# Attention ahead of two feed-forward blocks: the values' products of two query tiles issued together every second step

## Chip, cores and metric

One core of a Trainium2 chip. The metric is the device time of one execution in microseconds; the median of three runs of the kernel before is 1003.15 us (1000.76 to 1003.25).

## What is computed

Four batches of eight heads, 576 positions, head dimension 64, everything in float32. Then two feed-forward blocks on the 2304 x 512 result.

```python
scores = q @ k.T / sqrt(64)                      # causal
scores += minimum(-(cum_i - cum_j), 0)           # cum = cumsum(max(s, 0))
attn = exp(scores - rowmax) / (rowsum + 1e-9)
x = (attn @ v)                                   # heads side by side: 2304 x 512
h = maximum(x @ w_in, 0);  x = (h * h) @ w_out   # first block, d_ff 2048
h = x @ w2_in;  out = (h * cos(h)) @ w2_out      # second block
```

## The kernel before

The tokens are cut into nine blocks of 256 queries (`ORDER`, `_segments`). The attention of block k+1 runs beside the first feed-forward block of block k: that is the loop `for k in range(NB1)`, and each of its passes is a *step*. A **unit** is a segment of queries of one batch; a **job** is one tile of at most 128 queries of one head. There are 160 jobs. Jobs 0 to 31 (heads below `EARLY`) take another path, with float32 products and transpositions by TensorE, and are not touched by the change. Jobs 32 to 159 are touched. Most units have two tiles a head, so that an even job is a head's first tile and the odd job behind it the second; jobs 48 to 55, 104 to 111 and 144 to 159 have one tile a head, a width of 576 keys, and there an even and an odd job are two heads that share an output tile. Jobs 48 to 55, 104 to 111 and the second tiles of jobs 56 to 71 and 112 to 127 have 64 queries, the others 128.

The order on each engine is the program order, written by `step(i)` (the tile framework adds semaphores alone; a tile's buffer is handed on when all that reads it is done). What happens to job j, by step:

- step j: scores on TensorE (`emit_qk`, L487 and L496) into one of three PSUM banks, two for 576 keys
- step j+1: mask and row minimum on VectorE (`emit_mask`, L510), exp on ScalarE (`emit_exp`, L527)
- step j+2: `emit_split`: VectorE writes the weights as a float16 high and low part into a tile `p` (L555, L559; where the width is no multiple of 128, GpSimd first clears the rest, L554), and SP's queue issues a DMA that transposes `p` into a tile `pt` (L565)
- step j+5 (`LAG`, `lag(i)`): `emit_pv`: the products of `pt` with the values on TensorE, three of 64 columns for each 128 keys (L590), into the PSUM bank `pvs`
- after a pair of heads is complete, in the next step: `evacuate` (VectorE divides by the row sums and reads `pvs`, `xp`, L630) and, at the step's end, `turn` (one or two transpositions on TensorE, L644)

Between these a step issues one or two *slots* of the feed-forward block: `g1` (12 products of 256 columns into `hps`, L844) or `g2` (12 into `y`, L873), with `gact` on ScalarE (L855 to L857) and `grest` on VectorE (L863, the tile `gl`) between the two. All these products and their weights are 4 bytes wide; those of L590 are 2 bytes wide. At a block's last `g2` the two halves of `y` are copied into two tiles `yst` (ScalarE and VectorE, L881), stored to DRAM from SP's queue (L882), and squared and summed on ScalarE (L884). The next block's first `g2` writes the same PSUM banks.

The buffers in question: `pt` has three; `p` has two, and from the end of the first weights' conversion every third job (i % 3 == 2) uses the single buffer `p3` in place of them (`p_tile`); the tag `stg` has two buffers of 2 KB per partition, used by the weights' conversion (before step 37 and again in the last block) and by the two `yst`.

How many steps block k gets follows from `unit_done`, which uses `lag`: block 1 runs from step 37, block 2 from step 55, block 3 from step 79. SP's queue carries, in program order, the transpositions, the loads of q and k (`raw`, L220), of the values (`vb`, L367) and the stores of `yst`.

Of the kernel before, what the change touches and what calls it, by code (L numbers as in the profile page):

```python
# [10 lines left out]
F16 = mybir.dt.float16  # L11
# [12 lines left out]
NF = DFF // 128  # L24
# [9 lines left out]
LAG = (3, 5)  # L34
# [62 lines left out]
EARLY = 16  # L97
# [17 lines left out]
def attention_moe_moe_kernel(  # L115
# [24 lines left out]
    wp = ctx.enter_context(tc.tile_pool(name="wp", bufs=1))  # L140
# [4 lines left out]
    at = at_stack.enter_context(tc.tile_pool(name="at", bufs=1, side="right"))  # L145
# [171 lines left out]
    jobs = []  # L317
# [9 lines left out]
    jd = {}  # L327
    xb = {}
    evq, xtq, xcq = [], [], []
    lag1, wrest = [], []  # L330
# [185 lines left out]
        j["sb"], j["nb"] = sb, nb[0:r, len(j["ps"]) - 1:len(j["ps"])]  # L516

    def p_tile(i):
        third = nw[2] >= 2 * NF and not wrest and i % 3 == 2
        return at.tile([128, 1280], F16, tag="p3" if third else "p", bufs=1 if third else 2, name="p")  # L520

    def emit_exp(i):
# [17 lines left out]
    def emit_split(i):  # L540
        n, ti, q, r = jobs[i]
        j = jd[i]
        w, sb = j["w"], j["sb"]
        cw = 128 * ((w + 127) // 128)
        if n < EARLY:
            pp = j["ps"][0][0][:, BT:BT + cw]
            pt = at.tile([128, 640], F32, tag="pt", bufs=3, name="pt1")
            (nc.scalar.copy if ti else nc.vector.tensor_copy)(pt[:, 0:w], pp)
            j["pt"] = pt
            yield  # L550
            return
        p = p_tile(i)
        if cw > w:
            nc.gpsimd.memset(p[0:r, 0:2 * cw].rearrange("p (a c) -> p a c", a=2)[:, :, w:cw], 0.0)  # L554
        nc.vector.tensor_scalar(  # L555
            out=p[0:r, 0:w], in0=sb[0:r, 0:w], scalar1=PSC, scalar2=None, op0=ALU.mult
        )
        yield
        nc.vector.scalar_tensor_tensor(  # L559
            out=p[0:r, cw:cw + w], in0=sb[0:r, 0:w], scalar=PSC, in1=p[0:r, 0:w],  # L560
            op0=ALU.mult, op1=ALU.subtract,
        )
        pt = at.tile([128, 1280], F16, tag="pt", bufs=3, name="pt")
        pt = pt[:, 0:2 * cw // 128 * r].rearrange("p (a r) -> p a r", r=r)
        nc.sync.dma_start_transpose(out=pt, in_=p[0:r, 0:2 * cw])  # L565
        j["pt"] = pt
        yield
# [106 lines left out]
    def job(i):  # L674
        return jobs[i] if 0 <= i < NJ else None

    def lag(i):
        return LAG[not job(i) or jobs[i][0] >= EARLY]

    def heads_ahead(i, *fs):  # L680
        if job(i) and jobs[i][1] == 0:
# [3 lines left out]
    def unit_done(u):  # L685
        return last_job[u] + lag(last_job[u]) + 3


    nw = [2, 0, 0]
    stq = [(wp, 3)]  # L690
    p3 = [0]
# [285 lines left out]
    def softmax_tail(i):  # L977
        if job(i - 1):
            yield from emit_mask(i - 1)
        for j in stage(2, i - 2):  # L980
            yield from emit_split(j)

    def step(moe=0, bits=0, attn=True):
# [37 lines left out]
        if attn:  # L1021
            for j in stage(0, i - 2):
                if jobs[j][1] == 0:
                    load_v(jobs[j][0])
            for j in stage(3, i - LAG[0]):
                if j > i - lag(j):
                    stages[3] -= 1
                    break
                emit_pv(j)
# [104 lines left out]
    while prog[0] < unit_done(0):  # L1134
        i = prog[0]
# [271 lines left out]
```

## Time and profile before

| what | value |
|---|---|
| median of the runs | 1003.15 us |
| the profiled execution | 1003.76 us, its span 1002.0 us |
| PE busy | 966.9 us (96%) |
| DVE, ACT busy | 723.9 us (72%), 655.5 us (65%) |
| products of L590 | 1296, 61.2 us busy, from 122.9 to 559.6 us |
| transpositions by DMA, L565 | 128 |

Times in the profile count from the start of the span. PE is TensorE's matmuls, PEld its weight loads, DVE VectorE, ACT ScalarE, POOL GpSimd, SP the queue from which most DMAs are issued. In a timeline each row is a start, a duration, an engine, a line, an operation and its tiles; "x9" means nine in a row merged. [...]

### The profile page before, as it was taken

How to read it: one execution, taken by the hardware profiler on the slowest of the kernel's cores; microseconds unless marked ns; L12 is line 12 of the kernel's file. 1: busy time of each engine (PE TensorE's matmuls, PEld its weight loads, DVE VectorE, ACT ScalarE, POOL GpSimd, SP SyncE). 2: the span in 40 equal slices, each digit the busy share in tenths (PEclk: the TensorE clock that was granted, in tenths of full speed). 3: DMA queues.
4: the chain of work that ended last, by engine and by line, in shares of the span. 5: the costliest groups of instructions: out<-in, count | busy, mean ns of one | idle time of the engine just before them, and what ended most of it. 6: DMA issues, size and time to landing. Idle time of an engine off the chain costs nothing.

```text
span 1002.0 us, 20487 instructions
## 1 busy us (share of the span) xinstructions
PE 966.9 (96%) x7266; PEld 740.6 (74%) x7266; DVE 723.9 (72%) x1865; ACT 655.5 (65%) x1596; POOL 163.2 (16%) x258
## 2 busy tenths in 40 slices
PE   5999899999999999999999999999999999999998
PEld 4788898899999998999999997444544454444444
DVE  6879788867777897787888267798887545555555
ACT  4789777767777777767776578777766444433433
POOL 2000011111111121111211023330033341000000
PEclk9999999999999999999999999999999999999999
DMA  8955599746887986467898569210000000011001
GB/s 268 292 182 181 118 202 203 170 111 157 196 162 160 178 193 175 109 155 145 192 206 180 188 237 360 95 43 1 1 1 1 0 1 1 0 43 43 23 20 64
DMA packets 150711, 126.65 MB, mean 126 GB/s; under 512 B 108048, under 2 KB 125792, under 8 KB 150608
## 3 DMA queue, kind: packets, MB, share of 16 engines
q1 hardware_dynamic: 146688, 119.05, 46.1%
q0 software_dynamic: 3904, 6.29, 2.5%
q8 instruction: 57, 0.93, 0.4%
q14 instruction: 46, 0.38, 0.1%
q10 hardware_dynamic: 16, 0.01, 0.0%
HBM read 85.25 MB, written 15.81 MB: 101 GB/s over the span
## 4 chain that ended last, share of the span: by engine, by line
PE 79%; DVE 8%; DMA 6%; ACT 4%; issue 2%; SPq 1%; DVEq 0%; ACTq 0%
PE hps L844 18%; PE y L873 18%; PE o L1285 17%; PE hp L1230 17%; PE qkp L496 4%; PE pvs L590 4%; DMA rw<-in_w_dram 3%; DMA raw<-in_qk_dram 1%; PE xps L644 1%; DVE st L716 1%; DVE sb L510 1%; DVE gl L863 1%; DVE wt L737 0%; DVE k L357 0%; SPq L178 0%
## 5 line engine op out<-in xcount | busy, mean ns | idle before, releaser
L844 PE MATMUL hps<-xh,wt 128*128 128x256 f32 x1152 | 241.4, 292 | 4.1 <-ACT g L855 4.0
L873 PE MATMUL y<-gh,wt 128*128 128x256 f32 x1152 | 237.7, 289 | 0.0
L844 PEld LDWEIGHTS hps<-xh,wt 128*128 128x128 f32 x1152 | 191.7, 194 | 7.0 <-ACT g L855 5.5
L873 PEld LDWEIGHTS y<-gh,wt 128*128 128x128 f32 x1152 | 189.9, 192 | 1.3
L1230 PE MATMUL hp<-yh,wt 128*128 128x512 f16 (+1 forms) x640 | 185.9, 358 | 0.0
L1285 PE MATMUL o<-wt,gh 128*128 128x512 f16 x576 | 171.3, 379 | 2.0 <-ACT wt L1300 1.9
L873 PE MATMUL y<-gl,wt 128*128 128x256 f32 x576 | 163.4, 284 | 2.6 <-DVE gl L863 2.6
L844 PE MATMUL hps<-xl,wt 128*128 128x256 f32 x576 | 164.3, 285 | 0.9 <-DVE xl L661 0.9
L1230 PEld LDWEIGHTS <-wt 128*128 128x128 f16 x960 | 92.2, 98 | 93.3
L1242 ACT ACTIVATE a<-hp,hsc 128x512 f32<-128x512 f32 (+1 forms) x80 | 51.4, 643 | 118.6 <-PE hp L1230 117.2
L855 ACT ACTIVATE g<-hps 128x256 f32<-128x256 f32 x144 | 54.6, 379 | 107.7 <-PE hps L844 105.8
L1230 PE MATMUL hp<-yl,wt 128*128 128x512 f16 (+1 forms) x320 | 114.4, 358 | 0.0
L873 PEld LDWEIGHTS y<-gl,wt 128*128 128x128 f32 x576 | 110.6, 192 | 3.7 <-DVE gl L863 3.1
L844 PEld LDWEIGHTS hps<-xl,wt 128*128 128x128 f32 x576 | 111.7, 194 | 1.4 <-DVE xl L661 1.1
L1285 PE MATMUL o<-wt,gl 128*128 128x512 f16 x288 | 109.2, 379 | 0.4 <-DVE gl L1272 0.4
L1243 DVE TENSOR_SCALAR kf<-a 128x512 f32<-128x512 f32 (+1 forms) x80 | 34.5, 431 | 103.8 <-ACT a L1242 103.4
L1285 PEld LDWEIGHTS <-gh 128*128 128x128 f16 x576 | 56.2, 98 | 66.7 <-issue 2.4
L527 ACT ACTIVATE sb<-sb,nb 128x128 f32<-128x128 f32 (+8 forms) x160 | 93.7, 586 | 12.1 <-DVE nb L510 12.0
L339 POOL DMA_DIRECT2D k<-ext_d x80 | 40.8, 510 | 341.9 <-ACT g L856 92.3
L510 DVE CUSTOM_DVE_ANT_0 sb<-qkp,mask 128x128 f32<-128x128 f32 (+8 forms) x160 | 72.7, 454 | 13.8 <-PE qkp L487 8.6
L1251 ACT ACTIVATE a<-kf 128x512 f32<-128x512 f32 (+1 forms) x80 | 46.8, 585 | 46.6 <-DVE kf L1244 46.1
L559 DVE SCALAR_TENSOR_TENSOR p<-sb,p 128x512 f16<-128x512 f32 (+7 forms) x128 | 72.4, 565 | 4.0
(119 smaller groups left out, 1680.1 us busy)
## 6 DMA issues: line engine op xcount, KB each, us to landing
rw<-in_w_dram SPq DMA_DIRECT2D x64, 512.0 KB
raw<-in_qk_dram SPq DMA_DIRECT2D x32, 352.0 KB
raw<-in_qk_dram SPq DMA_DIRECT2D x16, 384.0 KB
v_d<-vt SPq DMA_DIRECT2D x16, 320.0 KB
raw<-in_qk_dram SPq DMA_DIRECT2D x16, 320.0 KB
vb<-v_d SPq DMA_DIRECT2D x32, 160.0 KB
vr<-in_v_dram POOLq DMA_DIRECT2D x15, 320.0 KB, 4.7
y_d<-yst SPq DMA_DIRECT2D x18, 256.0 KB
```

The lines of the kernel that those rows point to most:

```text
L339: nc.gpsimd.dma_start(out=hd[n][1][64:68, BT - nq:BT + nl], in_=ext_d[n, :, BT - nq:BT + nl])
L496: nc.tensor.matmul(p[0:r, 0:cn], m[0:kk, qo:qo + r], m[0:kk, BT + c0:BT + c0 + cn], start=(kk == 128), stop=(kk == 68),)
L510: nc.vector.tensor_tensor_reduce(out=sb[0:r, c0:c0 + cn], in0=p[0:r, 0:cn], in1=mask[0:r, mo + c0:mo + c0 + cn], scale=-0.125, scalar=(3.0 ...
L527: nc.scalar.activation(out=sb[0:r, 0:w], in_=sb[0:r, 0:w], func=ACTF.Exp, scale=-1.0, bias=j["nb"], accum_out=pd[n - h % 2]["z"][0:r, ti, ...
L559: nc.vector.scalar_tensor_tensor(out=p[0:r, cw:cw + w], in0=sb[0:r, 0:w], scalar=PSC, in1=p[0:r, 0:w], op0=ALU.mult, op1=ALU.subtract,)
L844: nc.tensor.matmul(hp, w[:, a, c * 128:(c + 1) * 128], (xh, xl)[e][:, c, :], start=(n == 0), stop=(n == 3 * KD - 1),)
L855: nc.scalar.activation(out=g, in_=hp, func=ACTF.Relu)
L873: nc.tensor.matmul(yps[k][d // 2][:, d % 2, :], w[:, a, d * 128:(d + 1) * 128], (gh, gl)[e], start=(f == 0 and n == 0 and d % 2 == 0), sto ...
L1230: nc.tensor.matmul(hp, w[:, a, c * 128:(c + 1) * 128], (yh, yl)[e][:, c, :], start=(m == 0), stop=(m == 3 * KD - 1),)
L1242: nc.scalar.activation(out=a, in_=hp, func=ACTF.Copy, scale=sm["hsc"][:, j, f:f + 1], bias=0.25)
L1251: nc.scalar.activation(out=a, in_=kf, func=ACTF.Sin, scale=-6.2831850)
L1285: nc.tensor.matmul(ops[j][a], (gh, gl)[e][:, a * 128:(a + 1) * 128], w[:, x, :], start=(first and m == 0), stop=(last and m == 2),)
```

## The change

`lag` is five for an even job and four for an odd one (it was five for both), so that the products of jobs 2m and 2m+1 are both issued at the end of step 2m+5, the odd job's directly behind the even one's. The odd job's come one step earlier than before. Steps of even number issue none. Since the last job of every unit is odd, each unit is done one step earlier: block 1 has 18 steps (it had 19), the later blocks as many as before.

Three of four jobs use the three buffers of `pt`, so that a buffer comes round after four jobs. Jobs with i % 4 == 3 take theirs elsewhere: in `p3` where the keys fill more than 512 columns, else in `stg`. `p_tile` no longer takes `p3` for jobs of 576 keys.

```diff
--- before.py
+++ after.py
@@ -516,7 +516,7 @@
         j["sb"], j["nb"] = sb, nb[0:r, len(j["ps"]) - 1:len(j["ps"])]
 
     def p_tile(i):
-        third = nw[2] >= 2 * NF and not wrest and i % 3 == 2
+        third = nw[2] >= 2 * NF and not wrest and i % 3 == 2 and jd[i]["w"] <= 512
         return at.tile([128, 1280], F16, tag="p3" if third else "p", bufs=1 if third else 2, name="p")
 
     def emit_exp(i):
@@ -560,7 +560,12 @@
             out=p[0:r, cw:cw + w], in0=sb[0:r, 0:w], scalar=PSC, in1=p[0:r, 0:w],
             op0=ALU.mult, op1=ALU.subtract,
         )
-        pt = at.tile([128, 1280], F16, tag="pt", bufs=3, name="pt")
+        if i % 4 < 3:
+            pt = at.tile([128, 1280], F16, tag="pt", bufs=3, name="pt")
+        elif cw > 512:
+            pt = at.tile([128, 1280], F16, tag="p3", bufs=1, name="pt3")
+        else:
+            pt = wp.tile([128, 1024], F16, tag="stg", bufs=2, name="pt4")
         pt = pt[:, 0:2 * cw // 128 * r].rearrange("p (a r) -> p a r", r=r)
         nc.sync.dma_start_transpose(out=pt, in_=p[0:r, 0:2 * cw])
         j["pt"] = pt
@@ -675,7 +680,9 @@
         return jobs[i] if 0 <= i < NJ else None
 
     def lag(i):
-        return LAG[not job(i) or jobs[i][0] >= EARLY]
+        if job(i) and jobs[i][0] < EARLY:
+            return LAG[0]
+        return LAG[1] - (i % 2 if job(i) else 0)
 
     def heads_ahead(i, *fs):
         if job(i) and jobs[i][1] == 0:
```

## Rows read from the trace of the kernel before

**Rows 1.** The page of the profile: the span and the busy line.

```profile
span 1002.0 us, 20487 instructions
...
PE 966.9 (96%) x7266; PEld 740.6 (74%) x7266; DVE 723.9 (72%) x1865; ACT 655.5 (65%) x1596; POOL 163.2 (16%) x258
```

**Rows 2.** Busy time by stretch: us, then busy (instructions) per engine, PEclk, DMA.

```profile
150.00:200.00 50.00, 45.80 (x445) 42.12 (x445) 43.33 (x128) 36.60 (x102) 8.84 (x21) 0.97 0.83 187
196.50:199.50 3.00, 3.00 (x16) 3.00 (x17) 2.63 (x11) 1.34 (x4) 0.37 (x1) 0.52 1.02 306
200.00:250.00 50.00, 50.00 (x461) 46.26 (x460) 35.37 (x143) 36.20 (x113) 8.30 (x22) 1.00 0.54 134
```

**Rows 3.** Timeline of PE, steady stretch: start, duration, engine, line, operation, tiles.

```profile
301.78 0.28 PE L844 MATMUL hps<-xh,wt 128*128 128x256 f32 x1
301.90 0.43 PE L590 MATMUL pvs<-vb,pt 128*128 128x64 f16 x9
302.17 0.36 PE L873 MATMUL y<-gh,wt 128*128 128x256 f32 x1
302.38 0.28 PE L873 MATMUL y<-gl,wt 128*128 128x256 f32 x1
```

**Rows 4.** Timeline of PE, tiles of 64 queries.

```profile
200.90 0.28 PE L873 MATMUL y<-gh,wt 128*128 128x256 f32 x1
201.11 0.66 PE L590 MATMUL pvs<-vb,pt 128*64 128x64 f16 x15
201.70 0.38 PE L844 MATMUL hps<-xh,wt 128*128 128x256 f32 x1
201.92 0.28 PE L844 MATMUL hps<-xl,wt 128*128 128x256 f32 x1
```

**Rows 5.** Waits of SP's queue: total us, times, longest.

```profile
SPq L565 <- PE pvs L590: 81.5, 71, 3.9
```

**Rows 6.** Timeline of PE, two products that waited; idle time in brackets.

```profile
195.55 0.63 PE L590 MATMUL pvs<-vb,pt 128*64 128x64 f16 x15 [1.39 <-DVE xp L630]
...
387.27 0.63 PE L590 MATMUL pvs<-vb,pt 128*64 128x64 f16 x15 [1.11 <-DVE xp L630]
```

**Rows 7.** Timeline of PE, unit 8.

```profile
523.34 0.39 PE L844 MATMUL hps<-xh,wt 128*128 128x256 f32 x1 [1.40 <-ACT g L855]
```

**Rows 8.** Timelines of ACT, DVE and PE at step 37.

```profile
122.39 0.59 ACT L881 COPY yst<-y 128x512 f32<-128x512 f32 x1 [0.31 <-PE y L873]
123.01 0.63 ACT L884 ACTIVATE yj<-yst 128x512 bf16<-128x512 f32 x1
...
123.89 0.63 ACT L884 ACTIVATE yj<-yst 128x512 bf16<-128x512 f32 x1 [0.16 <-DVE yst L881]
...
123.11 0.69 DVE L881 COPY yst<-y 128x512 f32<-128x512 f32 x1 [3.72 <-PE y L873]
...
127.48 0.39 PE L844 MATMUL hps<-xh,wt 128*128 128x256 f32 x1 [0.47 <-ACT g L855]
```

**Rows 9.** Timelines of SP and POOL: a transposition issued, its landing awaited.

```profile
193.24 1.33 SPq L565 DMA_TRANSPOSE pt<-p  x1
...
197.62 0.37 POOL L554 MEMSET p<- 64x128 f16 x1 [2.44 <-DMA pt<-p]
```

**Rows 10.** Timelines of SP and PE, jobs 36 and 37.

```profile
131.12 4.06 SPq L565 DMA_TRANSPOSE pt<-p  x2
...
135.38 0.44 PE L590 MATMUL pvs<-vb,pt 128*128 128x64 f16 x9
...
139.14 0.52 PE L590 MATMUL pvs<-vb,pt 128*128 128x64 f16 x12
```

**Rows 11.** Timelines of DVE and PE, jobs 54 to 56.

```profile
197.64 0.21 DVE L555 TENSOR_SCALAR p<-sb 128x128 f16<-128x128 f32 x1
...
203.56 0.66 PE L590 MATMUL pvs<-vb,pt 128*64 128x64 f16 x15
...
206.44 0.66 PE L590 MATMUL pvs<-vb,pt 128*64 128x64 f16 x15
```

## Prediction

> **What bounds the kernel now.** I read the page first: TensorE is busy for 966.9 of 1002.0 us [rows 1]. That number alone proves little, since its matmuls overlap, so I read the busy time by stretch next. [...] The timeline of PE then shows what a product costs: its distance to the next start. A product of 256 columns takes 0.12 us (301.78 to 301.90), nine products of L590 take 0.27 us (301.90 to 302.17, 0.03 each) [rows 3]. Last I read who waits: SP's queue, PE's idle times, and the places where the change gives a buffer to a second kind of tile.
>
> **Fewer returns from the short products.** The first long product behind a group of L590 takes 0.21 us (302.17 to 302.38) in place of 0.12 [rows 3]: 0.09 us a return. I read this as its weights, which the 0.03 us of the last short product cannot cover. With 128 jobs issued in 64 pairs, 64 returns go. By the order in the code, 24 of them lead into a long product (every second even job of the units with two tiles a head): 24 x 0.09 = 2.2 us. The other 40 lead into the transpositions of `turn`, which the change leaves standing between long products. There part of the 0.09 us stays, since a transposition is short too and its own return is still paid. Of these, 32 have tiles of 128 queries: 0 to 0.09 each, taken at 0.02, near zero because the long product's return behind a transposition remains: 0.6 us (0 to 2.9). Eight have tiles of 64 queries, where the way in costs as well: 200.90 to 201.11 is 0.21 us, and the way out 0.22 [rows 4]. That is 0.09 + 0.10 at most; the way in goes for certain: 0.09 to 0.19 each, taken at 0.12: 1.0 us (0.7 to 1.5). Together 3.8 us (2.9 to 6.6). The number of products is unchanged.
>
> [...]
>
> **Two waits that lose their cause.** At 195.55 and 387.27 us PE sat idle for 1.39 and 1.11 us before a group of L590, until DVE had read `pvs` (L630) [rows 6]. Both are at tiles of 576 keys, where before the change a pair of heads is read out in the same step in which the next job's products are issued. After it, the read-out falls in an even step and the next products at the end of the odd step behind it, a whole step later. 2.5 us go (0 to 2.5, the lower end if DVE is then late for another reason). [...]
>
> **SP's queue stands less.** With three buffers the transposition of job j waits for the products of job j-3, which are issued later in the same step: 71 waits, 81.5 us, 1.15 us each [rows 5]. With four, job j waits for job j-4, done a step or two before. So transpositions, and the loads queued behind them on SP, start about 1 us earlier. Most of that is hidden. Where it is not: at 523.34 us PE had waited 1.40 us for ACT [rows 7]; I put it to a late load of q and k. I take 1.0 us (0 to 1.4).
>
> **The borrowed `stg` at step 37.** Job 35 takes one of the two `stg` buffers in step 37, and its products come in step 39. In step 37 the first block's `y` is copied to two `yst`. The first takes the other buffer; the second cannot wait for job 35, because the `g2` that needs the freed PSUM banks stands ahead of job 35's products on PE. It has to wait for the first `yst` to be squared and stored. Before, the copies began at 122.39 (ACT) and 123.11 (DVE) [rows 8]. The square of the first ends at about 123.7 (123.01 + 0.63 and its sum): 0.6 us later than DVE began. The store can begin at 122.98; how long it takes no row tells. The nearest landing that a row shows is a transposition issued at 193.24, awaited until 197.62: 4.4 us [rows 9]. That makes a DVE copy at up to 127.4, 4.3 us late. ACT's second square stands in its order behind that copy, and everything of ACT behind the square; PE already waits for ACT at 127.48, 0.47 us long [rows 8], so there is no cover. Cost 0.6 to 4.3 us; I take 2.4, between ends of which neither is nearer in kind. Blocks 3, 4 and 6 copy while job 75, 91 or 131 holds `stg`, but there these products come at the end of the same step, ahead of the next `g2`: about 1 us of DVE's time, beside PE's work, 0.
>
> **Odd jobs one step earlier.** Their transposed tile must have landed when the even job's products end. The tightest row is job 37: its transposition was issued at 131.12, and the even job 36 ends its products at 135.7 (135.38 and nine times 0.03), 4.6 us later; job 37's own began at 139.14 [rows 10]. With a landing after 4.4 us [rows 9] nothing is lost; if it landed only just before 139.14, 3.4 us. I take 1.0 (0 to 3.4), the lower end being nearer. Elsewhere a step of 2.9 to 3.8 us between two groups [rows 10, 11] and the earlier issue leave enough: 0.
>
> **`p3` held past its turn.** Job 55 (576 keys) keeps its transposed tile in `p3` until its products in step 59; job 56 wants `p3` for `p` in step 58. DVE then stands, with its masks, `gl` and read-outs queued behind, from 197.64 until job 55's products, which follow job 54's: 203.56 + 2 x 0.59 = 204.7 [rows 4, 11]. That is up to 7.1 us of DVE's time by the old clock. What PE issues in these two steps (two slots of 12 x 0.12 = 1.44 us, two pairs of scores, the products: some 4.6 us) needs only what DVE made before, because `grest` is issued about three steps ahead of its `g2`. So PE loses little if it then finds DVE no more than that behind: 0 to 7.1 us. Job 113 stands the same way behind job 111, but within one step, 0 to 2.4 us. Both together I take at 1.4 us, near the lower end, since after 200 us DVE has 35.37 us of work in 50 [rows 2] and catches up. The two-buffer `p` at 576 keys costs 0: job j-2's transposition was issued two steps before.
>
> **Sum.** -3.8 - 2.5 - 0.5 - 1.0 + 2.4 + 1.0 + 1.4 = -3.0 us. Block 1's lost step changes nothing by itself, since its slots stay. On the profiled execution (1003.76 us, 1.8 more than its span) this gives 1000.8; that one lies 0.6 above the median of 1003.15, to which I forecast 1000.2 us.
>
> **Rivals.**
> - *The gain is real but given back.* Step 37 at 4.3 and job 37 at 3.4 us take 4.3 us more than I did, and the net is +1.3, with the earlier SP queue and the clock still in: 1004.5. For it: no cover at 127.48 [rows 8]. Against: one place each.
> - *DVE's stop at `p3` reaches PE.* If PE needs something from DVE before its two steps of 4.6 us end, it stands until DVE has come through what it did in the old trace from 197.64 to 203.66. The stop is then 7.1 us on PE's time, and with 2.4 at job 113 the sum is -3.0 - 1.4 + 9.5 = +5.1: 1008. It decides at a stop longer than PE's own 4.6 us. For it: from 150 to 200 us DVE is busy for 43.33 of 50 us [rows 2]. Against: what stands behind on DVE is used two or three steps later.
> [...]
> - *More than forecast.* Step 37 at 0.6, the `p3` stops and job 37 hidden: -3.0 - 1.8 - 2.4 = -7.2, and with returns at 5 us -8.4: 995.
>
> **Chances.** My forecast (995.5 to 1001.5) 0.45, more than that 0.08, given back 0.22, returns not smaller 0.05, `p3` reaching PE 0.20. The measurement tells 0.3%, 3 us, from no change. Of the forecast's own cases, which lie around that bound, some four in five are faster: with the case of more, 0.45 faster; 0.33 within, 0.22 slower (all of `p3`, little of the rest). The range reaches into `p3`: 994.5 to 1006.5.
>
> **What would show it.** Groups of L590 twice as long at every second step, one 0.21 us return each; the idle times at 195.55 and 387.27 gone; SP's waits for L590 far below 81.5 us; the second `yst` copy on DVE 0.6 to 4.3 us later than its turn at step 37, and PE idle behind it; DVE idle before job 56's L555 until L590. Wrong would be: PE idle before the odd job's products in many pairs, or PE idle for more than 2 us behind job 56.

## The result, and the profile after

The changed kernel takes 1008.58 us (median of 6 runs, 1005.86 to 1009.81) beside 1002.33 for the kernel before on the same chip: ratio 1.0064, 95% interval 1.0049 to 1.0080. It is slower; 1000.2 was forecast, and the range ended at 1006.5. The profiled execution took 1009.36 us, its span is 1007.6 [rows 1: 1002.0]; PE is busy for 964.6 us in place of 966.9, so PE has less to do and stands more. Below the change lines have moved: the products are L595 (were L590), the read-out L635 (L630), the transposition by DMA L570 (L565), that of the output tile L649 (L644), `g1` L851, `g2` L880, `gact` L862 to L864, `xl` L666, the copies, stores and squares of `yst` L888, L889, L891.

First the two places where PE stands. The rows are timelines: start, duration, engine, line, operation; in brackets the idle time before it and what ended it. Step 37, kernel after, on DVE, ACT and PE (before: [rows 8]):

```profile
123.19 0.69 DVE L888 COPY yst<-y 128x512 f32<-128x512 f32 x1 [4.29 <-DMA y_d<-yst]
...
123.92 0.63 ACT L891 ACTIVATE yj<-yst 128x512 bf16<-128x512 f32 x1 [2.17 <-DVE yst L888]
...
127.50 0.58 PE L851 MATMUL hps<-xh,wt 128*128 128x256 f32 x1 [2.50 <-ACT g L862]
```

ACT's first copy began at 120.40 and DVE's second should have followed 0.7 us later, as it did before; it waited for the store of the first. PE's idle time of 0.47 us became 2.50. Next, the border of blocks 1 and 2, on DVE, PE, ACT, SP and POOL (before: [rows 6, 9, 11]):

```profile
206.94 0.23 DVE L555 TENSOR_SCALAR p<-sb 128x128 f16<-128x128 f32 x1 [6.97 <-PE pvs L595]
...
209.35 0.21 DVE L666 TENSOR_TENSOR xl<-xps,xh 128x64 fp32r<-128x64 f32 x1
...
194.35 0.27 PE L649 MATMUL xps<-ident,xp 64*128 64x64 f32 x1 [1.11 <-DVE xp L635]
197.85 1.14 PE L595 MATMUL pvs<-vb,pt 128*64 128x64 f16 x30
204.33 0.63 PE L595 MATMUL pvs<-vb,pt 128*64 128x64 f16 x15 [1.41 <-DMA vb<-v_d]
205.88 0.96 PE L595 MATMUL pvs<-vb,pt 128*64 128x64 f16 x15 [0.92 <-DMA vb<-v_d]
209.61 0.59 PE L398 MATMUL xps<-ss,ones 128*128 128x2 f32 x2 [2.77 <-DVE xl L666]
...
208.90 0.40 ACT L527 ACTIVATE sb<-sb,nb 128x128 f32<-128x128 f32 x1 [5.53 <-DVE nb L510]
...
193.86 0.93 SPq L889 DMA_DIRECT2D y_d<-yst  x2
196.54 1.35 SPq L570 DMA_TRANSPOSE pt<-p  x1
197.94 0.59 SPq L367 DMA_DIRECT2D vb<-v_d  x1
198.63 0.38 SPq L220 DMA_DIRECT2D raw<-in_qk_dram  x1
199.19 3.33 SPq L570 DMA_TRANSPOSE pt<-p  x1
202.56 0.57 SPq L367 DMA_DIRECT2D vb<-v_d  x1
...
204.00 0.20 POOL L554 MEMSET p<- 64x128 f16 x1 [6.49 <-DMA pt<-p]
```

The reader is to see a chain. The tile and the values of job 54 leave SP at 196.54 and 197.94, behind two stores (193.86). Before, the tile left at 193.24 [rows 9], ahead of the same stores (196.05). POOL, which wants the buffer of `p` that this transposition reads, gets it at 204.00, 7.5 us after the issue; the products can start only at 204.33, when the values are there. Job 55's come at 205.88. DVE, which wants `p3` for job 56, stands until they are done: 6.97 us. Behind that stop on DVE is `xl` (209.35), which must read the bank `xps` before PE may write into it (L398, the sums of the values' squares): 2.77 us more. What follows is at half the clock. Busy time by stretch, kernel after (us, then busy and instructions of PE, PEld, DVE, ACT, POOL; PEclk; DMA):

```profile
126.80:130.40 3.60, 2.90 (x13) 2.90 (x14) 3.43 (x8) 2.19 (x7) 0.73 (x1) 0.54 0.57 139
200.00:206.00 6.00, 3.67 (x41) 3.30 (x40) 0.00 (x0) 3.20 (x12) 0.71 (x2) 0.97 0.81 137
205.40:215.60 10.20, 6.95 (x41) 6.58 (x42) 5.81 (x26) 3.73 (x12) 0.20 (x1) 0.51 0.32 79
```

For 10.2 us the clock is granted at 0.51, behind a stretch in which PE was busy for 3.67 us of 6, with the two waits for `vb` of 1.41 and 0.92 us in it. The products of 256 columns then start 0.22 us apart (210.42 to 210.64), where 0.12 was measured in a stretch at 1.00 [rows 3]. Before, the 3 us from 196.5 had 0.52 here [rows 2].

What the two places cost together is read from the start of one same product, the first `g1` product near 223 us of the kernel before, and of another 137 us later, in which stretch PE waits for next to nothing. Before, then after:

```profile
222.98 0.39 PE L844 MATMUL hps<-xh,wt 128*128 128x256 f32 x1
...
360.88 0.28 PE L844 MATMUL hps<-xh,wt 128*128 128x256 f32 x1
```

```profile
229.19 0.37 PE L851 MATMUL hps<-xh,wt 128*128 128x256 f32 x1
...
366.10 0.28 PE L851 MATMUL hps<-xh,wt 128*128 128x256 f32 x1
```

At 223 us the kernel is 6.21 us behind. Just ahead of the first product that the change moves it had been 1.94 us ahead:

```profile
121.42 0.34 PE L873 MATMUL y<-gh,wt 128*128 128x256 f32 x1
```

```profile
119.48 0.29 PE L880 MATMUL y<-gh,wt 128*128 128x256 f32 x1
```

Up to there the change does nothing that PE could gain by; the profiled execution before had lost time at half the clock (see the last section). So in these two executions the two places lose 8.15 us. From 223 to 361 us it takes 136.91 us in place of 137.90, with 20 groups of L595 in place of 40. Not all of these 0.99 us are returns. Since the blocks start a step earlier, the stretch holds the scores of one job of 576 keys less (four products, 0.54 us, by 506.52 to 507.06) and of one job of 256 columns more (two, 0.24 us), so that 0.30 us of work has moved out of it. Of waits (us in total, times, longest), the ones that the prediction named, after (SP before: [rows 5]):

```profile
SPq L570 <- PE pvs L595: 4.8, 5, 1.1
```

```profile
PE xps L649 <- DVE xp L635: 3.0, 4, 1.1
...
PE pvs L595 <- DMA vb<-v_d: 2.3, 2, 1.4
```

SP's waits for the products are gone. PE's waits for `xp` are not: they were 2.5 us before the products and 0.6 before the transposition, and are 3.0 us before the transposition (L649) alone.

### The profile page after: what moved, and what is told of

It reads as the page before. It is cut to its first block, busy times and chain, and to the rows that moved or that the text cites. A ratio compares the mean times of both kernels' runs of the same rounds, so it can differ in the third digit from the quotient of the medians.

```text
span 1007.6 us, 20476 instructions
## 1 busy us (share of the span) xinstructions
PE 964.6 (96%) x7266; PEld 741.2 (74%) x7266; DVE 722.0 (72%) x1865; ACT 654.4 (65%) x1596; POOL 161.8 (16%) x258
## 4 chain that ended last, share of the span: by engine, by line
PE 41%; DVE 4%; ACT 3%; DMA 2%; issue 1%; SPq 0%; DVEq 0%; POOL 0%; ACTq 0%; POOLq 0%
PE o L1292 17%; PE hp L1237 17%; PE y L880 3%; PE hps L851 3%; DMA pt<-p 1%; DMA raw<-in_qk_dram 1%; DVE wt L747 1%; DVE kf L1251 0%; PE pvs L595 0%; DVE a L1264 0%; ACT wt L738 0%; PE qkp L496 0%; DVE kf L1250 0%; ACT st L713 0%; ACT a L1249 0%
## 5 line engine op out<-in xcount | busy, mean ns | idle before, releaser
L851 PE MATMUL hps<-xh,wt 128*128 128x256 f32 x1152 | 241.0, 292 | 3.8 <-ACT g L862 3.7
L880 PE MATMUL y<-gh,wt 128*128 128x256 f32 x1152 | 237.0, 289 | 0.0
L851 PEld LDWEIGHTS hps<-xh,wt 128*128 128x128 f32 x1152 | 192.5, 194 | 6.5 <-ACT g L862 5.3
L880 PEld LDWEIGHTS y<-gh,wt 128*128 128x128 f32 x1152 | 189.8, 192 | 1.5
L880 PE MATMUL y<-gl,wt 128*128 128x256 f32 x576 | 163.6, 284 | 2.6 <-DVE gl L870 2.6
L851 PE MATMUL hps<-xl,wt 128*128 128x256 f32 x576 | 164.8, 286 | 0.9 <-DVE xl L666 0.9
L862 ACT ACTIVATE g<-hps 128x256 f32<-128x256 f32 x144 | 54.7, 380 | 107.5 <-PE hps L851 104.6
L880 PEld LDWEIGHTS y<-gl,wt 128*128 128x128 f32 x576 | 110.6, 192 | 3.7 <-DVE gl L870 3.1
L851 PEld LDWEIGHTS hps<-xl,wt 128*128 128x128 f32 x576 | 112.2, 195 | 1.5 <-DVE xl L666 1.1
L555 DVE TENSOR_SCALAR p<-sb 128x512 f16<-128x512 f32 (+7 forms) x128 | 46.5, 364 | 45.7 <-ACT sb L527 20.0
```

What stands on the lines that cost most here:

```text
L555: nc.vector.tensor_scalar(out=p[0:r, 0:w], in0=sb[0:r, 0:w], scalar1=PSC, scalar2=None, op0=ALU.mult)
L851: nc.tensor.matmul(hp, w[:, a, c * 128:(c + 1) * 128], (xh, xl)[e][:, c, :], start=(n == 0), stop=(n == 3 * KD - 1),)
L862: nc.scalar.activation(out=g, in_=hp, func=ACTF.Relu)
L880: nc.tensor.matmul(yps[k][d // 2][:, d % 2, :], w[:, a, d * 128:(d + 1) * 128], (gh, gl)[e], start=(f == 0 and n == 0 and d % 2 == 0), sto ...
```

## The experiments

Each was timed beside the kernel before, whose median was 1000.2 to 1000.5 us. "Without clock" is an estimate: the mean time less (1 - mean granted clock) x span, averaged over the runs. It takes off at most what was lost at half clock, and too much where PE stands idle at half clock (after, 207.40 to 209.00 us: busy for 0.00 us, clock 0.50). By that the kernel before has 998.3 to 998.8.

| kernel | ratio, 95% interval | mean clock | without clock |
|---|---|---|---|
| after | 1.0064 (1.0049 to 1.0080) | 0.9942 | 1002.5 |
| e1: job 56 not in `p3` | 1.0041 (1.0025 to 1.0057) | 0.9947 | 999.8 |
| e2: job 35 not in `stg` | 1.0045 (1.0030 to 1.0061) | 0.9950 | 1000.6 |
| e3: jobs 35, 56, 113 out of the way | 1.0007 (0.9995 to 1.0019) | 0.9972 | 998.8 |
| e4: pairing alone, three buffers | 1.0032 (1.0017 to 1.0047) | 0.9955 | 999.6 |
| e5: buffers alone, no pairing | 0.9989 (0.9977 to 1.0001) | 0.9983 | 997.6 |
| e6: e3, tiles of 64 queries unpaired | 1.0072 (1.0054 to 1.0090) | 0.9938 | 1001.9 |
| e7: e3, stores from GpSimd | 0.9991 (0.9979 to 1.0004) | 0.9985 | 998.6 |
| e8: before, stores from GpSimd | 1.0029 (1.0014 to 1.0044) | 0.9960 | 999.4 |
| e9: pairing, jobs 55, 111 in `stg` | 1.0030 (1.0014 to 1.0046) | 0.9959 | 1000.1 |
| e10: e9, tiles of 64 queries unpaired | 1.0021 (1.0003 to 1.0038) | 0.9965 | 999.8 |
| e11: buffers alone, 55, 111 in `stg` | 0.9983 (0.9967 to 0.9999) | 0.9981 | 997.5 |
| e12: e11, jobs 72 to 103 paired | 1.0050 (1.0034 to 1.0065) | 0.9948 | 999.8 |
| e13: e11, tiles of 64 queries paired | 1.0021 (1.0006 to 1.0037) | 0.9956 | 997.9 |
| e14: e11, last unit paired | 0.9997 (0.9983 to 1.0011) | 0.9976 | 997.6 |
| e15: e12, blocks start as in e11 | 0.9986 (0.9975 to 0.9997) | 0.9983 | 997.4 |
| e16: e9, blocks start as in e11 | 1.0056 (1.0041 to 1.0071) | 0.9933 | 999.7 |

**The borrowed buffers (e1 to e4).**

```diff
 e1, e3 (e1: i != 56 alone):
-        third = nw[2] >= 2 * NF and not wrest and i % 3 == 2 and jd[i]["w"] <= 512
+        third = nw[2] >= 2 * NF and not wrest and i % 3 == 2 and jd[i]["w"] <= 512 and i not in (56, 113)
 e2, e3:
-        if i % 4 < 3:
+        if i % 4 < 3 or i == 35:
 e4: p_tile and pt as in the kernel before, lag as in the change
```

> The changed kernel, but job 56 takes p and not p3, so that VectorE need not wait for job 55's products. Theory (the stop at p3 in step 58 costs the most): VectorE's 6.97 us of idle time before job 56's L555 and PE's waits of 1.41, 0.92 and 2.77 us behind it go, and so does the stretch at half clock behind them; about 7 us less than the changed kernel, a ratio to the kernel before near 0.999. Rival (the stop is covered, and the loss is spread over late transposed tiles or lies at step 37): less than 2 us change, a ratio of 1.005 or more.

> The changed kernel, but job 35's transposed tile takes the pt buffers, so that both copies of the first block's y find an stg buffer free in step 37. Theory: PE's idle time of about 2.5 us before an hps product near 127 us goes back to the 0.47 us of before, and the half-clock stretch behind it goes; about 3 us less than the changed kernel, a ratio near 1.003, with the stop at job 56 unchanged. Rival (the copy's lateness is absorbed before 200 us, since the next stretch waits for other things anyway): within 1 us of the changed kernel, 1.006.

> The changed kernel without the three collisions: job 35 in pt, jobs 56 and 113 in p. Theory (pairing saves about 0.09 us for each of 24 returns, some more elsewhere, and only the collisions cost): 3 us below the kernel before, a ratio near 0.997. Rival (pairing itself costs something, as odd jobs' tiles land late): at or above 1.000, with idle time of PE before odd jobs' products.

> The kernel before with the pairing alone: three pt buffers and p_tile as they were, no borrowed buffer. Every odd job's transposition then waits for the products of the job three before it, in the same step. Theory: the returns saved are the same 2 to 3 us, and a transposition still has two steps to land; a ratio of 0.997 to 0.999. Rival (the fourth buffer is needed): transpositions issued late land after the even job's products, PE idles before L590 in many pairs, a ratio above 1.003.

With all three jobs out of the way, 0.57% goes. Mending job 56 alone brings 0.23%, and 0.38% (with job 113) where job 35 is mended already; mending job 35 alone brings 0.19%, and 0.34% where job 56 is mended. In e2 step 37 is as before (PE's wait 0.48 us), in e1 it is as after (2.51); in e2 DVE's stop stays, and PE pays for it. PE in e2, then in e3, at the border:

```profile
202.60 0.96 PE L595 MATMUL pvs<-vb,pt 128*64 128x64 f16 x15 [1.96 <-DMA vb<-v_d]
206.33 0.59 PE L398 MATMUL xps<-ss,ones 128*128 128x2 f32 x2 [2.77 <-DVE xl L666]
```

```profile
202.26 0.63 PE L595 MATMUL pvs<-vb,pt 128*64 128x64 f16 x15 [0.73 <-DMA vb<-v_d]
219.44 0.38 PE L398 MATMUL xps<-ss,ones 128*128 128x2 f32 x2 [0.71 <-DVE xl L666]
```

From the `g1` product at 155.53 us to the one at 222.98 it takes 67.45 us before, and by the same products 72.29 after, 72.68 in e2, 67.57 in e1 and 65.48 in e3: in this stretch the loss hangs on job 56. e1 came out at 1.0041 all the same, where 0.999 had been expected. Step 37 remains in it, PE still waits for values at 204.15 and 205.78 (1.00 and 0.99 us), and DVE still stands before job 56, for 3.76 us, now until a transposition has landed; behind that stop PE waits for nothing that DVE makes.

So the collisions explain nearly all of the loss against the kernel before. They do not explain why e3 gains nothing, as its rival had it. e4 says that pairing with three buffers costs: in it PE waits 1.57 and 0.98 us at 203.81 and 205.42 for values that are late. Its rival named the ratio, but not the reason: many pairs were to wait, and four groups of L590 do.

**The other half, and two guesses at the border (e5 to e8).**

```diff
 e5 (e3's buffers; p3 kept from p where a tile may lie in it):
-        return LAG[1] - (i % 2 if job(i) else 0)
+        return LAG[1]
 e6 (on e3):
+        return LAG[1] - (i % 2 if job(i) and not 48 <= i < 56 and not 104 <= i < 112 else 0)
 e7 (on e3), e8 (on the kernel before):
-                nc.sync.dma_start(out=y_d[k, :, 2 * a:2 * a + 2, :], in_=st)
+                nc.gpsimd.dma_start(out=y_d[k, :, 2 * a:2 * a + 2, :], in_=st)
```

> The four buffers alone: each job's products keep their own step (lag five for all), job 35 keeps a buffer of pt, and p3 is not taken for p while a transposed tile may lie in it. With lag five and four buffers, job j waits for job j-4, whose products end a step or two before, so SP's waits for the products of pvs should be nearly gone. Theory (the queue's standing is hidden): ratio 0.999 to 1.001, the start of the feed-forward chunks follows the kernel before within 0.5 us outside half-clock stretches. Rival (the queue's standing was worth my 1.0 us or more, and pairing eats it): ratio 0.996 to 0.9985. Second rival (the moved buffers cost by themselves, since the tiles of 576 keys have two p in place of three): ratio above 1.002, with PE or DVE waiting for p or pt between 170 and 206 us and 365 and 405 us.

> The change without its three buffer collisions, and with lag five again for the odd jobs of the units with one tile a head (48 to 55, 104 to 111), so that only the units with two tiles a head are paired there. Theory (in those units the pairing takes away a step of landing time, the tiles of jobs 54 and 55 come late, and the idle time brings half the clock): the waits of PE before the products at 202 to 206 us go, ratio 0.996 to 0.999, about 2 us below the kernel with the collisions taken out alone (1.0007). Rival (the late tiles are made up for later in DVE's and ACT's slack, and the pairing gains nothing anywhere): 0.9995 to 1.002, no different from that kernel. The waits for xp at 195 and 387 us should be where they were in the kernel before, at the products, 1.1 to 1.4 us each.

> The change without its three buffer collisions, and with the stores of yst issued from GpSimd's queue in place of SP's. Theory (the transposed tiles of jobs 54 and 55 are late because they stand behind these stores on SP): these tiles land 1 to 2 us earlier, PE's waits of about 1 us before the products at 202 to 206 us shrink or go, ratio 0.997 to 0.9995. Rival (the tiles are late because DVE is late with p, or because the transfers themselves are slow beside the stores): the waits stay within 0.3 us, and the ratio at 1.000 to 1.002; if issuing from GpSimd holds back its memsets, worse.

> The kernel before with nothing changed but that the stores of yst are issued from GpSimd's queue. It tells what that edit does without pairing. Theory (without pairing the tiles have a step more to land, so the stores on SP's queue are hidden): 0.999 to 1.001. Rival (SP's queue counts in the kernel before as well): 0.996 to 0.9985.

e5 lies between theory and rival (0.9989): the four buffers without pairing do no harm, and whether they do good its interval, which ends at 1.0001, does not tell. e6 was expected to be the better kernel and is the worst of all. DVE and PE at the border:

```profile
204.06 0.23 DVE L555 TENSOR_SCALAR p<-sb 128x128 f16<-128x128 f32 x1 [3.35 <-ACT vt L390]
...
206.62 0.63 PE L595 MATMUL pvs<-vb,pt 128*64 128x64 f16 x15 [2.57 <-DVE xp L635]
```

Job 56 sent out of `p3` needs one of the two `p`, the one that job 54's transposition, issued at 197.04, reads. I put the wait to that landing: the profile names `vt` of ACT (done at 204.02), of which job 56 needs nothing. In e3 the same wait is 1.37 us long and is ended by the DMA `pt<-p` (DVE at 199.73). My mending of the `p3` collision had moved it. More of e6's loss lies later: from the `g1` product at 377.36 us (before) to the one at 404.90 it takes 33.78 us in place of 27.54, with waits of 1.85 and 2.16 us at 386.06 and 392.06. e12, below, loses in the same place. e7 missed its mechanism: PE's wait is 0.89 us there beside 0.73 in e3, so the place of the stores in SP's queue is not what makes the tiles late. Whether the transfers themselves do, no run tells. Its time is not above e3's; on the kernel before (e8) the same edit costs 0.29%. What of it gains in one and costs in the other stays open.

**Another home for the tiles (e9 to e11).**

```diff
 e9 (on the change), with 35 in pt; e11: lag five for all as well; e10: e9 with e6's lag
-        elif cw > 512:
+        elif cw > 512 and i not in (55, 111):
             pt = at.tile([128, 1280], F16, tag="p3", bufs=1, name="pt3")
```

> The change with its pairing everywhere, and its two collisions over p3 taken away in another way: the transposed tiles of jobs 55 and 111 lie in stg (64 queries need 1280 bytes of its 2 KB), so that jobs 56 and 113 can take p3 for p as in the kernel before; job 35 keeps a buffer of pt. Theory (where 56 and 113 were sent to the two buffers of p in place of p3, DVE stood for the landing of job 54's transposition, 1.37 us at 199.73, so the collision was only moved): DVE's idle time before job 56's L555 goes; PE's wait of 0.9 us for the landing of job 54 stays; ratio 0.998 to 1.0005. Rival (that wait of DVE cost nothing): 1.0000 to 1.0015, as the kernel with 35, 56 and 113 sent elsewhere (1.0007). Second rival (the two yst of block 1 now wait for job 55's stg, or the other way about): a copy on DVE or a transposition on SP late by more than 1 us near 195 or 390 us, ratio above 1.0015.

> The same, with lag five for the odd jobs of the units with one tile a head (48 to 55, 104 to 111). It is the kernel that came out at 1.0072, with one thing changed: jobs 56 and 113 take p3 for p and do not wait for the landing of the transposition of job 54 (6.9 us there) in one of two buffers of p. Theory (that kernel lost because DVE stood 3.35 us at 204.06 and PE then waited 2.57 us for xp at 206.62, and the like at 383 to 389): both waits go, ratio 0.996 to 0.999. Rival (the step of lag five beside lag four at the border of the units costs by itself): still above 1.003, with PE waiting 2 us or more near 203 and 385 us.

> The four buffers alone, lag five for all jobs, with the transposed tiles of 55 and 111 in stg and p3 free for jobs 56 and 113. SP's queue stands less and no collision is left. Theory (SP's standing was hidden but for the wait of ACT at 523.34): ratio 0.998 to 0.9995, that wait of 1.40 us shorter by 1 us or more, the rest as in the kernel before. Rival (pairing would have been worth its 3.8 us and this kernel lacks it): the paired kernels of this call are at least 0.2% below this one.

DVE's wait before job 56 is gone in e9, and the kernel is slower than e3 all the same: as the second rival had it, job 55's tile is late, and PE waits 2.00 us at 204.90 for its values. e10, expected at 0.996 to 0.999, mends e6's place at 203 us but keeps 1.41 and 1.63 us of waits at 379.64 and 386.54. e11 has the lowest ratio of the study, 0.9983. It lies below the change by the 0.8% between the two ratios, and below the kernel before by 1.75 us between the medians, which is at the edge of what can be told: its interval ends at 0.9999. Its only difference from e9 is the lag, that is, the pairing and with it the starts of the blocks: 1.0030 beside 0.9983, 5.3 us between the medians.

**Where pairing is paid (e12 to e16).**

```diff
 on e11, lag; e12: 72 <= i < 104; e13: 48 <= i < 56 or 104 <= i < 112; e14: 144 <= i < 160
-        return LAG[1]
+        return LAG[1] - (i % 2 if 72 <= i < 104 else 0)
 e15 (on e12), e16 (on e9), unit_done:
-        return last_job[u] + lag(last_job[u]) + 3
+        return last_job[u] + (LAG[1] if job(last_job[u]) and jobs[last_job[u]][0] >= EARLY else LAG[0]) + 3
```

> The kernel with four buffers and no collision, lag five for all (0.9983), and pairing put back for jobs 72 to 103 alone: two whole units with two tiles a head, where PE waits for nothing. It measures the returns by themselves. Theory (a return into a long product saves 0.09 us, one into a transposition about 0.02): eight returns into long products and eight into transpositions, 0.9 us less at the start of the chunks between 230 and 370 us beside the kernel without pairing; ratio 0.997 to 0.999. Rival (the returns save nothing): the chunks' starts keep within 0.3 us of it. Second rival (the unit's end one step early brings a wait at 365 to 405 us, as in the kernel in which the tiles of 576 keys alone had lag five): waits of 1.5 us or more there, ratio above 1.000.

> The same kernel with pairing put back for the units of 64 queries and 576 keys alone (jobs 48 to 55 and 104 to 111). Theory (what pairing costs without any collision of buffers is paid here, since the tiles of jobs 54 and 55 land late at the border of the blocks): waits of PE of 1 to 2 us before the products near 200 us, at half the clock behind them in most runs, 2 to 4 us in all; ratio 1.000 to 1.003. Rival (paid elsewhere): ratio 0.9975 to 0.9995 and no wait over 0.5 us before these products; the waits for xp near 190 and 380 us move from the products to the transposition of the output tile in either case.

> The same kernel with pairing put back for the last unit alone (jobs 144 to 159, 128 queries, 576 keys). Theory (the loads of q and k come late here when the products of two heads are issued together): DVE and ACT wait for raw and PE for hi and k between 525 and 550 us, 1.5 to 2 us lost there, against 0.7 us of returns; ratio 0.999 to 1.0005, about 1 us above the kernel without pairing. Rival (the 2 us of the paired kernels near 545 us come from their other units' pairing, which shifts the steps against the chunks): no loss there, ratio 0.9975 to 0.9985.

> Pairing for jobs 72 to 103 alone, as in the kernel that came out at 1.0050, but the end of a unit is counted with lag five for odd jobs too, so that the blocks start at the same steps as without pairing. Theory (that kernel lost some 7 us from 377 to 413 us because block 5 began a step earlier beside the tiles of 576 keys, not because of the pairs): the gain of 1.4 us by 368 us stays (0.09 us for each of 16 pairs), nothing is lost between 377 and 413, ratio 0.995 to 0.9985. Rival (the loss comes from lag four beside lag five at the border): waits of 1.4 us or more at 377 to 413 us as before, ratio above 1.002.

> Pairing for all touched jobs with no collision of buffers, as in the kernel that came out at 1.0030, but the blocks start at the same steps as without pairing. Theory (part of pairing's cost was the blocks' earlier start): the 2 us lost near 545 us go, and the losses at the borders near 200 and 397 us shrink to what the late landing of the transpositions of jobs 54 and 55 costs (1 to 3 us); ratio 0.997 to 1.001. Rival (the cost is the late landing and the half clock behind it alone): ratio 1.002 to 1.004.

e12 against e15 is the sharpest pair of the study: the same 16 pairs, but in e12 blocks 4 and 5 begin a step earlier, and the loss comes where block 5 begins. e12's second rival was right. PE's waits between 376 and 413 us, in e12 and then in e15:

```profile
378.50 0.32 PE L496 MATMUL qkp<-k 68*64 68x288 f32 x1 [1.16 <-DMA k<-ext_d]
384.49 0.59 PE L398 MATMUL xps<-ss,ones 128*128 128x2 f32 x2 [2.16 <-DVE xl L666]
412.55 0.25 PE L595 MATMUL pvs<-vb,pt 128*128 128x64 f16 x3 [1.47 <-DVE xp L635]
```

```profile
381.74 0.63 PE L595 MATMUL pvs<-vb,pt 128*64 128x64 f16 x15 [1.11 <-DVE xp L635]
```

The step's shift is the cause: 1.0050 beside 0.9986. How it acts I only argue: the early block puts its slots, its copies of `y` and its loads beside the tiles of 576 keys, where PE waits for DVE and for loads already. The returns themselves are measured where nothing else changes, from the same product near 217 us to the one near 355, in e11 and e15:

```profile
217.02 0.39 PE L851 MATMUL hps<-xh,wt 128*128 128x256 f32 x1
...
354.95 0.28 PE L851 MATMUL hps<-xh,wt 128*128 128x256 f32 x1
```

```profile
218.11 0.39 PE L851 MATMUL hps<-xh,wt 128*128 128x256 f32 x1
...
355.08 0.28 PE L851 MATMUL hps<-xh,wt 128*128 128x256 f32 x1
```

137.93 and 136.97: 0.96 us. Of the 16 pairs 15 lie in this stretch (25 groups in place of 40), the other products are the same, and 7 x 0.09 + 8 x 0.02 = 0.79 would be due. In times e15 and e11 do not differ (0.9986, 0.9983).

e13 loses as expected (1.0021), but not for the reason expected. Its SP and PE rows:

```profile
189.01 1.22 SPq L570 DMA_TRANSPOSE pt<-p  x1
...
191.41 2.41 SPq L889 DMA_DIRECT2D y_d<-yst  x2
196.96 1.21 SPq L570 DMA_TRANSPOSE pt<-p  x1
...
200.93 0.63 PE L595 MATMUL pvs<-vb,pt 128*64 128x64 f16 x15 [2.92 <-DMA vb<-v_d]
```

Job 55's transposition starts 8 us after job 54's, behind the stores that still read the `stg` it wants. Without pairing the same order is harmless (e11: 195.92, and no wait), because its products come a step later. In e16, with pairing everywhere and the old starts of the blocks, that wait is 3.19 us at 204.41 and 3.65 at 398.97. So `stg` is no free home for job 55 either, and e9's and e16's times hold a collision of their own: a paired kernel without any was not reached. e16 (1.0056) lies above its theory, above its rival, and above e9, from which only the blocks' starts tell it apart. Its two waits are longer than those of e9 (2.00 us at 204.90 and 1.11 at 398.63); whether that is all stays open. e14's rival was right in its reason: ACT waits for `raw`, 2.52 us at 532.54, and PE for nothing between 525 and 550 us. Its ratio, 0.9997, is the theory's, with an interval that covers both. The paired kernels lose near 545 us (after: ACT waits 2.39 us for `raw` at 545.83, PE 0.31 and 0.43 behind it). I put that to the shift of the blocks' starts. Two products, the same in each kernel, before, after and e11:

```profile
505.96 0.36 PE L844 MATMUL hps<-xh,wt 128*128 128x256 f32 x1
...
561.19 0.28 PE L844 MATMUL hps<-xh,wt 128*128 128x256 f32 x1
```

```profile
511.04 0.36 PE L851 MATMUL hps<-xh,wt 128*128 128x256 f32 x1
...
566.17 0.28 PE L851 MATMUL hps<-xh,wt 128*128 128x256 f32 x1
```

```profile
500.10 0.36 PE L851 MATMUL hps<-xh,wt 128*128 128x256 f32 x1
...
553.58 0.28 PE L851 MATMUL hps<-xh,wt 128*128 128x256 f32 x1
```

55.23, 55.13 and 53.48 us: the buffers gain 1.75 here, the change 0.10. Because its blocks start earlier, the change has one job's scores more in this stretch (0.54 us); on equal work it gains 0.64. With the old starts (in e14 all but block 8's) pairing keeps most of the gain: by the same products e14 gains 1.46 and e16 1.26. e9, which differs from e16 in the starts alone, takes 55.54 us with the same job more: 0.23 gained on equal work.

## Why the prediction was wrong

- **`p3` held past its turn (+1.4): the step that failed.** The stop was foreseen (7.1 us; 6.97 measured) and put at 1.4 us for both jobs, because what PE issues in these two steps "needs only what DVE made before". The list of what PE issues left out L398: it needs the bank that `xl` reads, `xl` stood behind the stop on DVE, and PE waited 2.77 us for it. What PE had queued did not cover the stop. By the times the place is worth 0.23% (change and e1) to 0.38% (e2 and e3), 2.3 to 3.8 us. Part of that is clock, which no term held: behind the stop PE is busy for 6.95 us at 0.51, worth an estimated 3.4 us (6.95 x 0.49). That is the rival "DVE's stop at `p3` reaches PE". That the time, 1008.58, fell on its 1008 is luck: it priced 9.5 us for the two stops, counted the two waits below as gone, and held nothing for late tiles. Job 113 cost nothing: DVE stood 1.60 us at 402.41 and PE did not wait.
- **Elsewhere the earlier issue leaves enough: 0.** It does not at jobs 54 and 55: 2.33 us of waits. The landing was judged by 4.4 us [rows 9], for a tile that left SP ahead of the stores; here the tile of the same job left behind them and took 7.5 us, 7.8 with the values behind it (196.54 to 204.33). Job 54 is even, and its own products did not move. It is the blocks' starts that put the stores ahead: with the old ones (e11, e13, e16) the tile leaves first, and these products wait for nothing. Behind the stores they wait 1.41 us in the change, 1.00 in e1 and 1.57 in e4, but not in e2, e3 and e9.
- **Two waits that lose their cause (-2.5): gained nothing.** I moved the products away from the read-out and forgot that `turn`, in the same step as the read-out, needs the same `xp`. The wait went one row down, from L590 to L649 (1.11 us at 194.35 and at 392.19). The sum's -0.5 stood for the half clock behind the first of these waits, and no run shows it as a gain: the 3 us from 196.5, granted 0.52 before [rows 2], had 1.00 after, but the 10.2 us from 205.4 had 0.51.
- **Block 1's lost step changes nothing: wrong.** The number of slots stays, but what they stand beside does not. e12 and e15 show what one step's shift can cost, 0.64%; in the change it takes back some 1.1 us between 506 and 561 us (0.64 gained on equal work in place of 1.75), beside the order of tile and stores above.
- **The borrowed `stg` (+2.4, 0.6 to 4.3): right.** DVE copied 2.79 us after ACT (120.40 to 123.19), 2.1 later than the 0.72 of before; PE lost 2.0 us of idle time and by estimate some 1.3 to the clock of 0.54 from 126.80 to 130.40 (0.46 x 2.90 us of busy time). By the times it is worth 0.19% (change and e2) to 0.34% (e1 and e3), 1.9 to 3.4 us.
- **Returns (-3.8): right** where measured: 0.96 us over 15 of the 64 pairs, where 0.79 was due. Behind the 21 products at 303.49 the next long ones start at 304.11 and 304.31, still 0.20 apart: a return is paid after the change too. The weight loads agree with the reading of the return as weights: before, those of the product at 302.17 begin at 302.15 on PEld, 0.02 us ahead of it, and those of the product at 302.38 at 302.26, 0.12 us ahead.
- **SP's queue (-1.0): right, and taken back in part.** 81.5 us of waits became 4.8, and the wait of 1.40 us at 523.34 [rows 7] is gone. e11, which has this and no pairing, keeps the gain of 1.75 us there; the change keeps 0.64.
- **Job 37 (+1.0): 0.** PE waited for no product there. With the old starts of the blocks it does: 0.80 us at 137.01 in e16.

The change was forecast at -3.0 us and came out at +6.2 beside the kernel before. By the sizes above, `p3` makes 0.9 to 2.4 us of the 9.2 between the two, the late tiles 2.3, the waits and the clock that were to go 3.0, and `stg` and SP's queue together -0.1 to 1.4; job 37 takes off 1.0. That is 5 to 8 us; the rest is not assigned.

## What to carry to other kernels

A borrowed buffer is priced by the longest hold of the lender at its worst step, and by what the waiting engine has queued behind that wait: list that queue to the first thing another engine needs, banks to be freed included. Moving a group of products one step earlier also moves every count that is derived from its lag, here the start of the blocks; change one and hold the other. When idle time of TensorE is priced, the half clock that may follow (here 0.51 for 10.2 us) belongs to the price.

## What was not expected of the hardware

Idle time of PE cost more than itself. In step 37 and at the border PE waited 7.60 us (2.50, 1.41, 0.92 and 2.77), and the half clock behind these waits (0.54 and 0.51) cost by estimate some 4.7 us of its busy time (0.46 x 2.90 + 0.49 x 6.95). But half clock does not follow each time. At 117 us, ahead of all that the change touches, PE waited 1.55 us for ACT in both kernels, and the clock fell in one execution and not in the other. Before, then after, with the busy time by stretch:

```profile
117.74 0.38 PE L398 MATMUL xps<-ss,ones 128*128 128x2 f32 x2 [1.55 <-ACT vt L390]
...
118.00:121.40 3.40, 3.40 (x16) 3.23 (x16) 1.22 (x4) 0.56 (x2) 0.00 (x0) 0.52 0.12 50
```

```profile
117.26 0.38 PE L398 MATMUL xps<-ss,ones 128*128 128x2 f32 x2 [1.55 <-ACT vt L390]
...
118.00:122.00 4.00, 4.00 (x49) 3.87 (x49) 0.90 (x3) 2.43 (x6) 0.51 (x1) 1.00 0.40 82
```

In the mean the change stands at 0.9942 of the full clock, the kernel before, as timed beside the experiments, at 0.9976 to 0.9984: (1 - 0.9942) x 1006.6 = 5.8 us against 1.6 to 2.4. So by this estimate at most 3.4 to 4.2 us of the loss are clock. Of the kernel before as it was timed beside the change itself no clock is on record; its profiled execution has 0.995. Executions of one kernel differ in the same way: those of the kernel before beside the experiments ran from 997.87 to 1005.87 us, with mean clocks of 0.993 to 1.000.

A transposition by DMA of one size, 64 x 1280, was awaited for 4.4 us [rows 9] in one place and for 7.5 us in another (196.54 to 204.00), there behind the stores of 2 x 256 KB and beside the loads of values, q and k.
